# A second buffer for one small exp, and ten more dummy matmuls, in a fused linear attention and MLP

## The chip, the cores and the metric

The kernel runs on one core of a Trainium2 chip. The metric is the device time of one execution in microseconds. TensorE (PE) does matrix products and transposes, ScalarE (ACT) the exp and GELU, VectorE (DVE) the other elementwise work, GpSimd (POOL) some casts and loads, and SyncE (SP) issues most transfers. Each engine works through its own instructions in the order in which they were written, and waits for another engine's semaphore where it needs its data or its buffer. The kernel before took 313.79 us, the median of three runs (313.42 to 314.2).

## The reference

```python
# q, k, v: (8 batches, 8 heads, 576 tokens, 64), float32
phi = lambda x: np.where(x > 0, x, np.exp(x) - 1) + 1      # = max(x, 0) + min(exp(x), 1)
kv  = einsum('bhsd,bhse->bhde', phi(k), v)                 # 64 x 64 per batch and head
z   = sum over the tokens of phi(k)
x   = (phi(q) @ kv) / (phi(q) @ z + 1e-6)                  # attention, all heads side by side: (4608, 512)
h   = x @ w_in                                             # 512 -> 2048
out = gelu_tanh(h) @ w_out                                 # 2048 -> 512, float32
```

## The kernel before

**Tiling.** Of the 576 tokens of a batch, 512 are its main part (128 partitions, 4 tokens each; one set of 128 tokens is called a chunk) and 64 are the rest. The rests of two batches form one group of 128 rows, so there are four groups, m = 0 to 3, of which the tiles are kr, vr and qr (k_r, v_r, q_r when loaded). The MLP runs over nine blocks of 512 tokens: j = 0 to 7 are the main parts, and the ninth is the four groups of rests. For each block `first_half(j)` computes h in 16 column tiles h_ps (L303, four matmuls of 512 columns each) and ScalarE applies GELU to each (L678). `second_half(j)` computes the output in 64 matmuls into four tiles o_ps (L721), which VectorE (L734, even chunks) and ScalarE (L736, odd chunks) copy to o_sb; two stores per block are issued on ScalarE's queue (L652).

**Attention of a batch.** ScalarE takes exp of k, of the resting k, of q and of the resting q (`exp_main` L167, `phi_rest` L189). VectorE makes phi of them (L172, L176) and casts v to vp (L204). PE computes kv_ps (L220, L228) head pair by head pair, five matmuls each; VectorE copies it to kvbd (L244). phi(q) is transposed to qt, by four transposing DMAs on SP's queue (L463, L615) for later batches, and on PE for the first two (L337, L249). Then the products n_ps (L255) follow, one per chunk, VectorE normalises each to x (L265, L267), and x is transposed to xt, either on PE (t_ps, L278, copied by ScalarE, L392) for batches 0, 1 and 2, or by DMA (L498). `first_half(j)` needs the whole of xt of its batch. The rests go the same way in `plan_rest` (qtr L512).

**Order around the change.** Attention of later batches is written into slots of the two MLP halves: `at(phase, j, slot, fn)` puts fn behind the matmuls of that slot. What matters here: in the second half of j = 1, slot 7 has the exps of k and q of batch 3, and then, from the line `at(2, 1, 7, ...)` near the end, the exp of resting q of group 1; slot 12 has the load of the GELU table; slots 13 to 15 have the transposes of batch 2's x on PE with ScalarE's copies to xt, in one order with the o_sb copies of j = 1. On VectorE, the phi of k of batch 3 is in slot 15 of that half; in the first half of j = 2, slot 0 has the cast of v, slot 1 the phi of q (and the transposing DMAs), slot 3 the phi of resting q of group 0, slots 4 to 7 the kv products of batch 3, slot 8 the phi of resting q of group 1, slots 11 to 14 the products with qt, slot 15 those of the resting group and the exps of batch 4. The exp of resting q of group 0 was done on ScalarE at the end of the first half of j = 1, with the exps of batch 2.

**Buffers.** The results of exp lie in the pool `pe` (L47), which has one buffer for each tile name. `phi_rest` (L186) names its tile after the tensor, so all groups of resting q share one tile, qr_e. The loaded q_r tiles lie in a pool with two buffers, as do the phi tiles.

**The first batch.** While its loads and exps run, PE is given dummy matmuls on a tile of zeros: `keep_warm(n)` (L326) issues 2n of them, 252 columns each (L329). The order on PE is: a group of 34, the transposes of the first two head pairs of q (L337), a group of 3, the transposes of the other two, a group of 1, the kv products of batch 0, a group of 1, and then the products and transposes of x with groups of 2 and 1 among them.

Of the kernel before, what the change touches and what calls it, by code (L numbers as in the profile page):

```python
# [9 lines left out]
BF16 = mybir.dt.bfloat16  # L10
# [5 lines left out]
def kernel(  # L16
# [14 lines left out]
    B, H, S, D = q.shape  # L31
    d_model, d_ff = moe_w_in.shape
    P = 128
# [13 lines left out]
    pe = ctx.enter_context(tc.tile_pool(name="pe", bufs=1))  # L47
# [122 lines left out]
    def phi_into(xp, x, e, hs):  # L170

        nc.vector.tensor_scalar(e[:, hs], e[:, hs], 1.0, None, op0=ALU.min)  # L172
        xv = x.rearrange("p h (c d) -> p c h d", d=D)
        ev = e.rearrange("p h (c d) -> p c h d", d=D)
        for c in range(xp.shape[1]):
            nc.vector.scalar_tensor_tensor(  # L176
                xp[:, c, hs, :], xv[:, c, hs, :], 0.0, ev[:, c, hs, :],
                op0=ALU.max, op1=ALU.add,
            )

    def phi_of(x, e, name):
        xp = pphi.tile([P, x.shape[2] // D, H, D], BF16, name=name)
        phi_into(xp, x, e, slice(0, H))
        return xp

    def phi_rest(name, m):  # L186
        x = ld[name, m]
        e = pe.tile([P, H, D], BF16, name=name + "_e")
        nc.scalar.activation(e, x, AF.Exp)  # L189
        return lambda: phi.__setitem__((name, m), phi_of(x, e, name + "_p"))  # L190

# [134 lines left out]
    def keep_warm(n):  # L326
        w_ps = ps_ho.tile([P, 512], FP32, name="w_ps", tag="ho")
        for _ in range(2 * n):
            nc.tensor.matmul(w_ps[:, 0:252], lhsT=warm[:, 0:P], rhs=warm)  # L329
# [3 lines left out]
    def transpose_q(i, copy):  # L333
        src = q_src(0)
        t_ps = ps_ho.tile([P, C, 2, P], BF16, name="t_ps", tag="ho")
        for c in range(C):
            nc.tensor.transpose(t_ps[:, c, 0, :], src(c, i), ident)  # L337
        copy(out=qt[:, :, i, :], in_=t_ps[:, :, 0, :])

    for n, e, s in (  # L340
# [7 lines left out]
            exp_rest_half(n, e, 0)  # L348
        else:
            nc.scalar.activation(e[:, s], ld[n, 0][:, s], AF.Exp)  # L350
    keep_warm(34)
    phi_into(kp, ld["k", 0], ke, halves[0])
    phi_into(kp, ld["k", 0], ke, halves[1])
    phi_into(qp, ld["q", 0], qe, halves[0])
# [1 line left out]
    cast_v(0, nc.scalar.copy, halves[0])  # L356
    for i in range(2):
        transpose_q(i, nc.scalar.copy)
    keep_warm(3)
    phi_into(qp, ld["q", 0], qe, halves[1])  # L360
    cast_v(0, nc.scalar.copy, halves[1])
    ke1 = exp_main("k", 1)
    cast_vr(0, (0,))
    for i in range(2, NP):
        transpose_q(i, nc.vector.tensor_copy)
    keep_warm(1)
    for i in range(NP):
        if i % 2 == 0:
            kv_ps = ps_a.tile([P, 2, 512], FP32, name="kv_ps", tag="a")
# [69 lines left out]
    def plan_prepare(b, exp_at, k_at, kr_at, v_at, q_at, qr_at, table_at):  # L439
# [3 lines left out]
        def exps():  # L443
            box["k"] = exp_main("k", b)
            if b % 2 == 0:
                box["kr"] = phi_rest("kr", b // 2)
            box["q"] = exp_main("q", b)
            if b % 2 == 0:
                box["qr"] = phi_rest("qr", b // 2)
# [143 lines left out]
    def plan_third():  # L593
# [4 lines left out]
        def exps():  # L598
            box["k"] = exp_main("k", b)
            box["kr"] = phi_rest("kr", 1)  # L600
            box["q"] = exp_main("q", b)
            box["qr"] = phi_rest("qr", 0)
            gelu_table()
# [193 lines left out]
```

## Time and profile before

| what | value |
|---|---|
| median of three runs | 313.79 us (313.42 to 314.2) |
| the profiled execution | 316.52 us, span 314.7 us |
| PE busy | 291.0 us, 92% of the span |
| ACT busy | 161.3 us, 51% |
| DVE busy | 132.1 us, 42% |
| POOL busy | 36.9 us, 12% |
| mean granted clock of TensorE | 0.962 |
| chain that ended last | PE 80%, DMA 7%, DVE 5%, ACT 4%, issue 3% |

The profile is of one execution. Busy shares are means over the span; the page also cuts the span into 40 slices of 7.87 us, in which a digit is the busy share in tenths. The chain that ended last is followed back from the last instruction, at each step to what released it. In a timeline a line is an instruction or a run of like ones; the brackets give the idle time of the engine before it and what ended it.

### The profile page before, as it was taken

The numbers are of one execution on the slowest core, as the hardware profiler recorded it, in microseconds if no ns is written. First come the engines' busy times: TensorE is split into PE (matmuls) and PEld (weight loads), VectorE is DVE, ScalarE is ACT, GpSimd is POOL, SyncE is SP. The second block draws the span as 40 slices with busy tenths as digits, with TensorE's granted clock in tenths as the row PEclk, the third lists the DMA queues.
The fourth block names the chain that finished last, engine by engine and source line by source line (L and its number), as shares of the span: only waits on it lengthen the run. The fifth ranks groups of instructions, "written<-read, shape, count | busy, mean of one in ns | idle before, by whom it ended". The sixth has DMA issues, their size and how long they took to land.

```text
span 314.7 us, 4258 instructions
## 1 busy us (share of the span) xinstructions
PE 291.0 (92%) x1651; PEld 150.8 (48%) x1680; DVE 132.1 (42%) x242; ACT 161.3 (51%) x223; POOL 36.9 (12%) x55
## 2 busy tenths in 40 slices
PE   8799999999813999989999999999999999999994
PEld 7566456544501454445445444544454444444443
DVE  3969685208790046924381459236433000000001
ACT  4757834789306468246825682567254036216500
POOL 7039558100005010000000000000000000000000
PEclk9969999999965799999999999999999999999999
DMA  7999899991678214992594468630613110011032
GB/s 247 346 391 390 308 387 338 334 332 27 196 263 210 92 42 93 358 256 55 157 357 123 61 218 307 120 67 28 160 30 69 67 67 0 2 67 67 2 67 68
DMA packets 64260, 53.24 MB, mean 169 GB/s; under 512 B 31728, under 2 KB 57584, under 8 KB 64240
## 3 DMA queue, kind: packets, MB, share of 16 engines
q1 hardware_dynamic: 60816, 41.82, 45.4%
q10 hardware_dynamic: 2464, 8.52, 7.2%
q0 software_dynamic: 960, 2.62, 3.1%
q8 instruction: 13, 0.21, 0.3%
q14 instruction: 7, 0.06, 0.0%
HBM read 36.70 MB, written 9.44 MB: 147 GB/s over the span
## 4 chain that ended last, share of the span: by engine, by line
PE 80%; DMA 7%; DVE 5%; ACT 4%; issue 3%; ACTq 0%; SPq 0%; DVEq 0%
PE h_ps L303 39%; PE o_ps L721 33%; DMA v_x<-in_v_dram 4%; PE n_ps L255 3%; PE kv_ps L220 3%; DMA q_x<-in_q_dram 2%; DVE q_p L176 1%; DMA out_dram<-o_sb 1%; ACT xt L392 1%; PE kv_ps L228 1%; DVE k_p L176 1%; PE w_ps L329 1%; PE t_ps L278 1%; ACT o_sb L736 1%; DVE q_e L172 0%
## 5 line engine op out<-in xcount | busy, mean ns | idle before, releaser
L303 PE MATMUL h_ps<-xt,w_in_sb 128*128 128x512 bf16 (+1 forms) x527 | 121.3, 374 | 3.9 <-ACT xt L392 2.2
L721 PE MATMUL o_ps<-w_out_sb,g 128*128 128x512 bf16 x545 | 123.5, 379 | 1.0 <-ACT w_out_sb L157 0.2
L678 ACT ACTIVATE g<-h_ps 128x512 bf16<-128x512 f32 x144 | 84.2, 598 | 53.0 <-PE h_ps L303 50.8
L303 PEld LDWEIGHTS <-w_in_sb 128*128 128x128 bf16 x604 | 57.8, 99 | 60.4 <-issue 7.3
L721 PEld LDWEIGHTS <-g 128*128 128x128 bf16 x560 | 54.1, 98 | 63.3 <-issue 0.5
L734 DVE COPY o_sb<-o_ps 128x512 f32<-128x512 f32 x17 | 11.7, 688 | 62.4 <-PE o_ps L721 62.3
L736 ACT COPY o_sb<-o_ps 128x512 f32<-128x512 f32 x18 | 10.6, 586 | 52.8 <-PE o_ps L721 52.8
L244 DVE CAST kvbd<-kv_ps 64x260 bf16<-64x260 f32 (+1 forms) x17 | 6.7, 395 | 47.8 <-PE kv_ps L228 47.7
L267 DVE TENSOR_TENSOR x<-n_ps,r 128x512 bf16<-128x512 f32 x36 | 24.9, 692 | 1.2
L176 DVE SCALAR_TENSOR_TENSOR k_p<-k_x,k_e 128x512 bf16<-128x512 f32 (+1 forms) x36 | 23.7, 721 | 0.3
L176 DVE SCALAR_TENSOR_TENSOR q_p<-q_x,q_e 128x512 bf16<-128x512 f32 (+1 forms) x40 | 23.0, 636 | 0.3
L172 DVE TENSOR_SCALAR k_e<-k_e 128x2048 bf16<-128x2048 bf16 (+1 forms) x9 | 5.9, 653 | 29.9 <-ACT k_e L167 25.3
L265 DVE RECIPROCAL r<-n_ps 128x8 f32<-128x8 f32 x36 | 7.4, 206 | 25.8 <-PE n_ps L255 25.8
L278 PE MATMUL t_ps<-ident,x 128*128 128x128 bf16 x48 | 5.3, 240 | 11.2 <-ACT o_sb L736 9.7
L167 ACT ACTIVATE k_e<-k_x 128x2048 bf16<-128x2048 f32 x7 | 13.4, 1910 | 2.1 <-DMA k_x<-in_k_dram 2.1
L255 PEld LDWEIGHTS <-qt 128*128 128x128 bf16 x128 | 10.3, 102 | 7.6 <-issue 1.1
L303 PE MATMUL h_ps<-xt_rest,w_in_sb 128*128 128x512 bf16 x63 | 13.9, 379 | 0.1
L255 PE MATMUL n_ps<-kvbd,qt 128*128 128x130 bf16 x128 | 13.2, 227 | 0.4 <-DVE kvbd L244 0.3
L329 PE MATMUL w_ps<-warm 128*128 128x252 bf16 x84 | 12.5, 310 | 1.1 <-DVE warm L128 1.1
L220 PE MATMUL kv_ps<-vp,k_p 128*128 128x130 bf16 x128 | 13.1, 231 | 0.0
L220 PEld LDWEIGHTS <-k_p 128*128 128x128 bf16 x128 | 10.1, 101 | 5.9
L146 ACT ACT_TABLE_LOAD x8 | 10.3, 1283 | 4.0 <-DVE o_sb L734 3.9
(58 smaller groups left out, 153.3 us busy)
## 6 DMA issues: line engine op xcount, KB each, us to landing
out_dram<-o_sb ACTq DMA_DIRECT2D x16, 512.0 KB, 4.3
k_x<-in_k_dram SPq DMA_DIRECT2D x7, 1024.0 KB, 6.0
v_x<-in_v_dram SPq DMA_DIRECT2D x7, 1024.0 KB, 11.8
q_x<-in_q_dram SPq DMA_DIRECT2D x6, 1024.0 KB, 7.9
w_st<-in_moe_w_out_dram SPq DMA_DIRECT2D x4, 1024.0 KB, 9.7
w_st<-in_moe_w_in_dram SPq DMA_DIRECT2D x3, 1024.0 KB, 9.4
q_x<-in_q_dram SPq DMA_DIRECT2D x4, 512.0 KB, 9.2
k_x<-in_k_dram SPq DMA_DIRECT2D x2, 512.0 KB, 4.1
```

Source lines behind the costliest of these rows:

```text
L146: nc.scalar.preload_act_table_set("gelu_apprx_tanh_and_others")
L167: nc.scalar.activation(e, ld[name, b], AF.Exp)
L176: nc.vector.scalar_tensor_tensor(xp[:, c, hs, :], xv[:, c, hs, :], 0.0, ev[:, c, hs, :], op0=ALU.max, op1=ALU.add,)
L220: nc.tensor.matmul(dst, lhsT=kp[:, c, P * i : P * (i + 1)], rhs=vps[b % 2][:, 2 * i : 2 * i + 2, c, :], start=(c == 0), stop=False,)
L255: nc.tensor.matmul(n_ps[rows, i // 2, 2 * E * (i % 2) : 2 * E * (i % 2) + 2 * E], lhsT=qt_c[:, i, rows], rhs=kvbd[:, i, :], skip_group_che ...
L267: nc.vector.tensor_tensor(x, n_v[:, :, :, 0:D], r[:, :, :, None].to_broadcast([P, 2, 4, D]), op=ALU.mult,)
L303: nc.tensor.matmul(h_ps[:, tok], lhsT=w_in_sb[:, c, P * m : P * (m + 1)], rhs=xt[:, c, tok], start=(c == 0), stop=(c == KM - 1), skip_grou ...
L329: nc.tensor.matmul(w_ps[:, 0:252], lhsT=warm[:, 0:P], rhs=warm)
L678: nc.scalar.activation(gs[j][:, i, :], ps, AF.Gelu_apprx_tanh)
L721: nc.tensor.matmul(o_pss[t], lhsT=g[:, m, P * t : P * (t + 1)], rhs=w_out_sb[:, m, :], start=(m == 0), stop=(m == MM - 1),)
L734: nc.vector.tensor_copy(dst, o_ps)
L736: nc.scalar.copy(dst, o_ps)
```

## The change

`phi_rest` names the exp tile of resting q after the parity of its group, qr_e0 or qr_e1; the name for resting k stays kr_e. Three calls of `keep_warm` in the first batch have larger counts: 34 becomes 36, 3 becomes 5, and 1 becomes 2 (the one ahead of the kv products of batch 0), which is ten matmuls of 252 columns more.

```diff
--- before.py
+++ after.py
@@ -185,7 +185,7 @@
 
     def phi_rest(name, m):
         x = ld[name, m]
-        e = pe.tile([P, H, D], BF16, name=name + "_e")
+        e = pe.tile([P, H, D], BF16, name=f"{name}_e{m % 2 if name == 'qr' else ''}")
         nc.scalar.activation(e, x, AF.Exp)
         return lambda: phi.__setitem__((name, m), phi_of(x, e, name + "_p"))
 
@@ -348,7 +348,7 @@
             exp_rest_half(n, e, 0)
         else:
             nc.scalar.activation(e[:, s], ld[n, 0][:, s], AF.Exp)
-    keep_warm(34)
+    keep_warm(36)
     phi_into(kp, ld["k", 0], ke, halves[0])
     phi_into(kp, ld["k", 0], ke, halves[1])
     phi_into(qp, ld["q", 0], qe, halves[0])
@@ -356,14 +356,14 @@
     cast_v(0, nc.scalar.copy, halves[0])
     for i in range(2):
         transpose_q(i, nc.scalar.copy)
-    keep_warm(3)
+    keep_warm(5)
     phi_into(qp, ld["q", 0], qe, halves[1])
     cast_v(0, nc.scalar.copy, halves[1])
     ke1 = exp_main("k", 1)
     cast_vr(0, (0,))
     for i in range(2, NP):
         transpose_q(i, nc.vector.tensor_copy)
-    keep_warm(1)
+    keep_warm(2)
     for i in range(NP):
         if i % 2 == 0:
             kv_ps = ps_a.tile([P, 2, 512], FP32, name="kv_ps", tag="a")
```

## Rows read from the trace of the kernel before

**Rows 1.** Page, 40 slices of the span: busy tenths of PE, and granted clock.
```profile
PE   8799999999813999989999999999999999999994
...
PEclk9969999999965799999999999999999999999999
```

**Rows 2.** Timeline of ScalarE, 79 to 101 us: start, duration, operation, count [idle before].
```profile
79.57 1.89 ACT L167 ACTIVATE q_e<-q_x 128x2048 bf16<-128x2048 f32 x1
94.61 0.63 ACT L189 ACTIVATE qr_e<-q_r 128x512 bf16<-128x512 f32 x1 [13.14 <-DVE qr_p L176]
...
97.16 0.34 ACTq L652 DMA_DIRECT2D out_dram<-o_sb  x1
...
98.50 0.60 ACT L736 COPY o_sb<-o_ps 128x512 f32<-128x512 f32 x1
```

**Rows 3.** Timeline of VectorE, the last phi of batch 3's work.
```profile
93.88 0.69 DVE L176 SCALAR_TENSOR_TENSOR qr_p<-q_r,qr_e 128x512 bf16<-128x512 f32 x1
```

**Rows 4.** Timeline of TensorE, 86 to 101 us.
```profile
86.29 0.38 PE L278 MATMUL t_ps<-ident,x 128*128 128x128 bf16 x4 [0.78 <-DVE o_sb L734]
86.51 1.03 PE L721 MATMUL o_ps<-w_out_sb,g 128*128 128x512 bf16 x4
...
100.65 0.59 PE L303 MATMUL h_ps<-xt,w_in_sb 128*128 128x512 bf16 x1 [1.88 <-ACT xt L392]
```

**Rows 5.** Chain that ended last, h_ps of batch 2: start, duration, what, count.
```profile
101.45 6.59 PE h_ps L303 x18
...
108.33 0.86 PE h_ps L303 x4
```

**Rows 6.** Windows of TensorE: length, busy (count), granted clock, DMA share, GB/s.
```profile
4.00:4.50 0.50, 0.50 (x5) 1.00 1.08 383
4.50:5.00 0.50, 0.50 (x7) 1.00 1.09 387
...
11.00:14.00 3.00, 2.02 (x15) 1.00 1.12 353
14.00:14.50 0.50, 0.34 (x3) 0.91 1.08 385
...
89.00:90.00 1.00, 0.00 (x0) 0.75 1.08 385
106.00:107.00 1.00, 1.00 (x4) 0.71 0.00 0
```

**Rows 7.** Tile q_r, 45 to 60 us: count, durations in ns, first and last start.
```profile
L76 POOL DMA_DIRECT2D q_r<-in_q_dram x4: 682/682/684, 49.5 to 51.5; - x4
```

**Rows 8.** Tile qt, 85 to 120 us: issues as in rows 7, and landing.
```profile
L463 SPq DMA_TRANSPOSE qt<-q_p x4: 1190/1216/1217, 91.9 to 95.8; - x4
...
DMA to landing us min/median/max: 2.3/3.0/4.7
```

**Rows 9.** Timeline of TensorE in the first batch.
```profile
11.96 0.81 PE L329 MATMUL w_ps<-warm 128*128 128x252 bf16 x6
13.39 1.72 PE L337 MATMUL t_ps<-ident,q_p 128*128 128x128 bf16 x8 [0.61 <-DVE q_p L176]
```

**Rows 10.** Chain that ended last: first batch, then kv of batch 1.
```profile
15.11 0.42 PE w_ps L329 x2
...
18.48 0.54 PE w_ps L329 x2
...
47.72 0.23 PE kv_ps L220 x4
```

**Rows 11.** Chain that ended last, 124 to 138 us.
```profile
124.87 13.03 DMA v_x<-in_v_dram
137.99 0.35 ACTq L652
```

**Rows 12.** Timeline of SyncE's queue, a load of batch 4.
```profile
82.36 1.26 SPq L67 DMA_DIRECT2D v_x<-in_v_dram  x1
```

**Rows 13.** Tile v_x, 20 to 160 us: landing of six loads.
```profile
DMA to landing us min/median/max: 9.7/12.4/17.4
```

## The prediction, made before the change was run

> **What bounds the kernel now.** I read the page's 40 slices first. PE is busy in nearly all of them and stands at 9 tenths or so to the end: after the first hundred microseconds the kernel is bound by TensorE's stream of matmuls [rows 1]. Two places break this. At about 87 to 102 us PE falls to 0 and 1 tenths and the granted clock to 5, and near 16 to 24 us the clock reads 6 while PE is busy (the two levels are 1.00, 2.4 GHz, and 0.50, 1.2 GHz; a slice between is a mean). What comes after is paced by PE, so time taken out of either place should reach the end.
>
> For the large hole I read ScalarE's timeline. It ends the exp of q of batch 3 at 81.46, then waits 13.14 us, until VectorE has finished qr_p, before a 0.63 us exp into qr_e; all that stands behind it in ScalarE's order waits too: a table load, the copy of o_sb, a store, the copies of xt [rows 2]. The qr_p waited for is the phi of the *first* group of resting q, 93.88 to 94.57, the last of VectorE's work for batch 3 [rows 3]. VectorE does not wait for ScalarE there; it is busy with that batch. So the wait is for the buffer qr_e: the exp of the second group may not overwrite the first group's before VectorE has read it.
>
> PE shows the price. Its last product of batch 1 ends at 87.54 and h_ps of batch 2 starts at 100.65, with only eight transposes between [rows 4]. That start is slow too: 18 matmuls take 6.59 us, against 0.86 for four later [rows 5], because the clock fell at about 89.5 and rose at about 106.6 [rows 6].
>
> **The second qr_e buffer.** It adds no instruction and removes none. Group m writes qr_e0 or qr_e1, so the exp at 94.61 no longer depends on the phi of group 0. Its input is no obstacle: the loads of q_r for both groups were issued from 49.5 to 51.5 [rows 7], 30 us ahead. Later groups meet a buffer whose phi ran two groups back, long done.
>
> Step by step. From the start of this exp to the o_sb copy of chunk 3 ScalarE took 98.50 - 94.61 = 3.89 us, all serial [rows 2]. Started at 81.50 it would be there at 85.4, so from now on PE holds it: the second set of transposes still waits for VectorE's copy of o_sb and ends at 86.67, and the last product of chunk 3 ends at 87.54 [rows 4]. From there the old pieces follow: 98.50 to 100.65 is 2.15 us for this o_sb copy, a store, two xt copies and the hand-over to PE. So h_ps starts at 87.54 + 0.04 (the hand-over) + 2.15 = 89.7 instead of 100.65: 10.95 us earlier. What is late next is this tail; the last two sets of transposes, 0.2 us each, run right behind 87.54, and PE then rests about 1.7 us.
>
> Does the rest follow? Phi, casts and transposes of batch 3 stay where they are, since VectorE was never held, but they are needed sooner. The kv products of batch 3 come after five groups of h_ps, 89.7 + 5 x 0.86 = 94.0; k_p and vp lie ahead of the qr_p that starts at 93.88 on VectorE [rows 3]. The products with qt come after 12 groups and four kv's of 0.29: 101.2. The transposing DMAs for them are issued at 91.9 to 95.8 and land within 4.7 us [rows 8]: the first by 96.6, the last by 100.5 with need at about 104.5. That cover of 4 us hides them; beyond it each microsecond of delay costs one. The loads of batch 4 now meet the two stores, 1 MB more at the 385 GB/s of the row of 89 to 90 [rows 6], 2.6 us: these loads are wanted only at the end of that h_ps stage, past 105, and the 2.6 us are inside the cover of 4.
>
> The clock: at full speed the 19 matmuls from 100.65 to 108.04 would take 19 x 0.215 = 4.1 instead of 7.4 us [rows 5], so up to 3.3 us come back. How much is the main uncertainty, as the new stop of 1.7 us might itself lose the clock. Bounds: nothing lost, or all 3.3. When PE goes dense at once with the clock down, the nearest row is the kernel's start: matmuls begin near 1.05 and their count per half microsecond goes from 5 to 7 at 4.5 [rows 6], so some 3.4 us at half speed (the clock's column shows 1.00 there all the same), a loss of 1.7. I take that if it falls. Would it? Before the fall at 14.4, PE was busy for 2.02 of the 3.00 us from 11 to 14 [rows 6], in pieces, with no stop over about 0.6 us [rows 9]. The new tail is emptier: a stop of 0.78, four products and twelve transposes, a stop of 1.7. By these rows it falls.
>
> The Trainium skill reads otherwise: "TensorE: Matmul & The Clock Gate", section "HAM oscillation — how this bites in real kernels", ties the fall to TensorE standing idle between bursts, and stops of 0.6 us would hardly count as that. By that rule the time is rival 1's, by the trace the forecast's; the fall at 14.4 speaks against the rule.
>
> Sum for this part: 10.95 + 3.3 - 1.7 = 12.55 us (without a new fall 14.25, with one as dear as the old 10.95).
>
> **The dummy matmuls.** keep_warm(n) issues 2n: four more in the first group, four in the second, two in the third. A group of six takes 0.81 us; taking 0.27 for the last, a step of one is 0.54 / 5 = 0.108, so four add 0.43. The second group's fall into the 0.61 us that PE waits for q_p ahead of 13.39 [rows 9]; the first group's into a like wait ahead of 10.67. Both are hidden, since VectorE's q_p sets those starts; if q_p came 0.4 earlier they would cost up to 0.4 each.
>
> The third is on the path, ahead of kv. If the clock falls at 14.4 as before, two more cost what two cost now, 0.42. If the filling keeps it up, four take 4 x 0.108 = 0.43, as two did, and the four kv's, 2.95 us from 15.53 to 18.48, take what they take in batch 1 at full speed, 0.23 for four matmuls and so 0.29 for five [rows 10]: 4 x 0.29 = 1.17, a gain of 1.8 that VectorE's chain behind it can follow whole. So -0.4 to +1.8. Neither end is nearer: little idle is left beside the dummies, but the transposes still come singly, at q_p's pace. I take the middle, 0.7.
>
> **Sum.** 12.55 + 0.7 = 13.25 us. The profiled execution took 316.52, its span 314.7 and 1.8 around it; the median of the timed runs, 313.79, is 2.7 below. I take the sum off the median: 300.5 (profiled, about 303.3).
>
> **Rivals.**
> 1. The wait goes and the clock holds over the new tail: 14.25 + 0.7 = 14.95, time 298.8. For it: PE is dense up to 85.5 and again from 89.7. Against it: the fall at 14.4.
> 2. The wait moves to a store. At 137.99 ScalarE issues a store only once v_x, issued at 124.87, has landed 13.03 us later [rows 11]; in the program's order that store is the eighth transfer after this v_x on the SP and ACT queues (four qt, a store, two qtr, this store). If the first store of batch 1, now ready at about 85, stood so behind batch 4's v_x, issued at 82.36 [rows 12], then with the shortest landing of a v_x, 9.7 us [rows 13], it would go out at 92.1 instead of 97.16 [rows 2]: 5.1 us gained, 308.7. With the longest, 17.4, it goes out at 99.8, 2.6 us later than before: 316.4, slower. It decides from a landing of 14.8. Against it: counted the same way, this store's eighth predecessor is a store of batch 0, landed long since.
> 3. The exp still waits, for something else that VectorE's last phi stands for: then only the dummies act, 313.1 (312.0 to 314.2). Against it: the two share nothing else.
> 4. The next stage meets late transposes: a delay of 7 us instead of the 4 that are covered gives 3 back, 303.5.
>
> **Chances.** Forecast 0.46, rival 1 0.40, rival 2 0.05, rival 3 0.03, rival 4 0.06. The forecast's own range is 299.4 to 303.2 (dummies +1.8 to -0.4, clock loss 1.7 to 3.3); rival 1 spans 297.7 to 299.9. The range 297.8 to 302.8 leaves out the tails and rivals 2 to 4. About 0.3% is what a measurement can tell from no change. Faster: the forecast, rivals 1 and 4, most of 2, some of 3: 0.95. Same: the middle of rival 3, 0.02. Slower: the long landings of rival 2, and the rest of rival 3, 0.03.
>
> **What would show it.** ScalarE's exp into the second qr_e directly behind that of q at about 81.5; PE's hole cut to about 1.7 us and h_ps of batch 2 starting near 89.7 (near 88 if the first batch gains its 1.8). The granted clock in the microseconds after 89 tells the forecast from rival 1; the clock between 14.5 and 21, and kv at 0.29 or 0.74 us a piece, tell the dummies' sign. The prediction is wrong if ScalarE waits elsewhere between 82 and 88, or if a new PE wait stands ahead of the kv or qt products of batch 3.

## The result, and the profile after

The changed kernel takes 298.94 us, the median of four runs (298.67 to 299.23), against 314.0 us for the kernel before (313.42 to 316.13): a ratio of 0.9509, with a 95% interval from 0.9463 to 0.9555. That is 15.1 us less. The forecast was 300.5 in a range from 297.8 to 302.8; the time lies in the range, and at the first rival's 298.8. Two runs that fell in a slower state of the chip, one of e1 (380.16 us at a mean granted clock of 0.75) and one of the kernel before in the same set (317.08), are left out of the figures below.

The page's 40 slices of the kernel after answer to [rows 1]. The two low slices of PE, whose digits are 1 and 3 there (the prediction read 0 and 1), are gone, and the granted clock reads 9 throughout.

```profile
PE   8989999999979999999999999999999999999994
...
PEclk9999999999999999999999999999999999999999
```

ScalarE's timeline after, the answer to [rows 2] (start, duration, operation, count, idle before). The exp into the second qr_e follows the exp of q at once, and nothing waits 13 us; the copy of o_sb of chunk 1 now waits for PE, and no longer stands behind an exp that waits for VectorE.

```profile
77.54 1.89 ACT L167 ACTIVATE q_e<-q_x 128x2048 bf16<-128x2048 f32 x1
79.34 0.61 ACT L189 ACTIVATE qr_e<-q_r 128x512 bf16<-128x512 f32 x1
...
82.19 0.59 ACT L736 COPY o_sb<-o_ps 128x512 f32<-128x512 f32 x1 [0.94 <-PE o_ps L721]
...
84.60 0.59 ACT L736 COPY o_sb<-o_ps 128x512 f32<-128x512 f32 x1 [0.28 <-PE o_ps L721]
```

VectorE's last phi of batch 3, the answer to [rows 3], starts at 91.84 against 93.88: VectorE's work stands where it stood but for the 2.04 us that the first batch gave. The wait was not shifted to VectorE; it fell away. (The first row is VectorE's copy of o_sb of chunk 2, which is needed further down.)

```profile
83.51 0.69 DVE L734 COPY o_sb<-o_ps 128x512 f32<-128x512 f32 x1
...
91.84 0.69 DVE L176 SCALAR_TENSOR_TENSOR qr_p<-q_r,qr_e 128x512 bf16<-128x512 f32 x1
```

TensorE's timeline after, the answer to [rows 4]. The second set of transposes, 83.31, has no stop ahead of it (0.78 us before), the last product ends at 84.56, the last eight transposes run behind it, and the stop ahead of h_ps of batch 2 is 1.71 us.

```profile
83.31 0.39 PE L278 MATMUL t_ps<-ident,x 128*128 128x128 bf16 x4
83.53 1.03 PE L721 MATMUL o_ps<-w_out_sb,g 128*128 128x512 bf16 x4
84.40 0.61 PE L278 MATMUL t_ps<-ident,x 128*128 128x128 bf16 x8
86.72 4.48 PE L303 MATMUL h_ps<-xt,w_in_sb 128*128 128x512 bf16 x19 [1.71 <-ACT xt L392]
```

The chain that ended last, the answer to [rows 5]: 18 matmuls of h_ps take 4.05 us instead of 6.59, at 0.86 for four from the start.

```profile
87.15 4.05 PE h_ps L303 x18
...
91.49 0.86 PE h_ps L303 x4
```

PE's dearest waits in the whole span after (in total, times, longest): 1.7 us is the tail of batch 1, 1.1 the start of the kernel, and the rest is below a microsecond each.

```profile
PE h_ps L303 <- ACT xt L392: 2.1, 2, 1.7
PE w_ps L329 <- DVE warm L128: 1.1, 1, 1.1
PE t_ps L278 <- DVE x L267: 0.6, 2, 0.4
```

Read against the profile before, the gain comes in five places. The two profiles differ by 17.8 us (316.52 to 298.75), the medians by 15.1; that is taken up below.

| point on PE | before | after | earlier by | new at this point |
|---|---|---|---|---|
| first h_ps of batch 0 | 22.80 | 20.76 | 2.04 | 2.04, first batch |
| first transposes of x of batch 2 | 84.26 | 82.23 | 2.03 | none |
| end of the last o_ps of batch 1 | 87.54 | 84.56 | 2.98 | 0.95, of which 0.78 is PE's stop for VectorE's o_sb |
| first h_ps of batch 2 | 100.65 | 86.72 | 13.93 | 10.95, ScalarE's wait |
| first kv of batch 3 | 108.04 | 91.20 | 16.84 | 2.91, the clock behind the wait |
| end of the span | 314.7 | 297.0 | 17.7 | 0.9, of which 0.80 is one PE wait for a gelu near 139 |

The last place is the wait of [rows 11]. ScalarE's timeline after still shows the store issued late, at 120.26, though the o_sb copy ahead of it ended at 117.70, and the next gelu held up by v_x; but PE no longer waits for that gelu (its list of waits has no such row). This wait varies from profile to profile, 0.80 and 0.21 us in the two of the kernel before, 0.32 in e1 and 0.51 in e10, which have the second buffer, and none in the two of the changed kernel; that the change takes it away is not shown.

```profile
120.26 0.34 ACTq L652 DMA_DIRECT2D out_dram<-o_sb  x1
120.64 2.56 ACT L678 ACTIVATE g<-h_ps 128x512 bf16<-128x512 f32 x5 [2.95 <-DMA v_x<-in_v_dram]
```

### The profile page after: what moved, and what is told of

The parts are those of the page before. It is cut to its first block, busy times and chain, and to the rows that moved or that the text cites. A ratio compares the mean times of both kernels' runs of the same rounds, so it can differ in the third digit from the quotient of the medians.

```text
span 297.0 us, 4281 instructions
## 1 busy us (share of the span) xinstructions
PE 286.2 (96%) x1661; PEld 149.4 (50%) x1690; DVE 131.9 (44%) x242; ACT 161.3 (54%) x223; POOL 37.3 (13%) x55
## 4 chain that ended last, share of the span: by engine, by line
PE 89%; DMA 3%; DVE 3%; ACT 2%; issue 1%; SPq 1%; ACTq 0%; DVEq 0%
PE h_ps L303 42%; PE o_ps L721 40%; PE n_ps L255 3%; PE kv_ps L220 3%; DMA k_r<-in_k_dram 3%; DMA out_dram<-o_sb 1%; PE kv_ps L228 1%; DVE x L267 1%; SPq L67 1%; DVE kvbd L244 1%; ACT xt L392 1%; PE t_ps L278 1%; DVE q_p L176 0%; ACT o_sb L736 0%; ACT w_out_sb L157 0%
## 5 line engine op out<-in xcount | busy, mean ns | idle before, releaser
L303 PE MATMUL h_ps<-xt,w_in_sb 128*128 128x512 bf16 (+1 forms) x527 | 118.5, 367 | 2.7 <-ACT xt L392 2.1
L303 PEld LDWEIGHTS <-w_in_sb 128*128 128x128 bf16 x604 | 57.0, 97 | 57.2 <-issue 2.3
L329 PE MATMUL w_ps<-warm 128*128 128x252 bf16 x94 | 13.6, 308 | 1.1 <-DVE warm L128 1.1
L167 ACT ACTIVATE k_e<-k_x 128x2048 bf16<-128x2048 f32 x7 | 13.4, 1910 | 2.0 <-DMA k_x<-in_k_dram 2.0
L303 PE MATMUL h_ps<-xt_rest,w_in_sb 128*128 128x512 bf16 x63 | 13.9, 379 | 0.1
L220 PEld LDWEIGHTS <-k_p 128*128 128x128 bf16 x128 | 9.5, 97 | 5.6
L220 PE MATMUL kv_ps<-vp,k_p 128*128 128x130 bf16 x128 | 12.2, 220 | 0.0
L150 POOL CAST w_in_sb<-w_st 128x1024 bf16<-128x1024 f32 x8 | 10.1, 1288 | 14.2 <-DMA w_st<-in_moe_w_in_dram 14.2
```

Source lines behind the costliest of these rows:

```text
L167: nc.scalar.activation(e, ld[name, b], AF.Exp)
L220: nc.tensor.matmul(dst, lhsT=kp[:, c, P * i : P * (i + 1)], rhs=vps[b % 2][:, 2 * i : 2 * i + 2, c, :], start=(c == 0), stop=False,)
L303: nc.tensor.matmul(h_ps[:, tok], lhsT=w_in_sb[:, c, P * m : P * (m + 1)], rhs=xt[:, c, tok], start=(c == 0), stop=(c == KM - 1), skip_grou ...
```

## The experiments

Each was run beside the kernel before on the same chip. Ratios are to that kernel in the same set of runs. The edits are shown against the changed kernel, that of e3 against the kernel before.

**e1, the buffer alone.**

```diff
-    keep_warm(36)
+    keep_warm(34)
...
-    keep_warm(5)
+    keep_warm(3)
...
-    keep_warm(2)
+    keep_warm(1)
```

> The second qr_e buffer alone, dummy matmuls at 34, 3, 1 as before. Theory: the buffer takes ScalarE's wait away by itself, and the dummies are worth about 2 us only because they keep the clock up in the first batch. Then ScalarE's exp into the second qr_e follows the exp of q at once, PE's stop ahead of h_ps of batch 2 is about 1.7 us as in the changed kernel, and the time is 301.0 (298.9 + 2.0). Rival, the dummies give nothing in the timed runs: 298.9 to 299.1. Rival, the clock falls again in the tail of batch 1 once the first batch is slow: about 302.7. In all three the h_ps stage of batch 2 starts some 12 us earlier than before relative to the last o_ps of batch 1.

Measured: 300.72 us, the median of five runs (299.86 to 301.91), ratio 0.9551 (0.9508 to 0.9595), so 13.9 us of the change come from this line alone (314.6 for the kernel before in this set). TensorE's timeline of this kernel has the same tail as the changed one, 2.3 us later: no stop ahead of the second set of transposes, 1.72 us ahead of h_ps, and h_ps at full speed. The clock did not fall in the tail.

```profile
85.62 0.39 PE L278 MATMUL t_ps<-ident,x 128*128 128x128 bf16 x4
...
86.71 0.61 PE L278 MATMUL t_ps<-ident,x 128*128 128x128 bf16 x8
89.03 4.48 PE L303 MATMUL h_ps<-xt,w_in_sb 128*128 128x512 bf16 x20 [1.72 <-ACT xt L392]
```

In the first batch of this profile the clock was down (window of TensorE: length, busy, granted clock, DMA share, GB/s), and this run took 301.43 us against the 301.0 expected for that. By the mean granted clock of each run the five split into two groups: 299.86 to 300.72 us at 0.993 to 1.000, and 301.43 and 301.91 at 0.986 and 0.985.

```profile
14.50:17.50 3.00, 2.93 (x20) 0.50 1.12 323
```

**e2, the dummies alone.**

```diff
-        e = pe.tile([P, H, D], BF16, name=f"{name}_e{m % 2 if name == 'qr' else ''}")
+        e = pe.tile([P, H, D], BF16, name=name + "_e")
```

> The ten dummy matmuls alone, one qr_e buffer. Theory: the clock stays at 1.00 in the first batch (kv 0.5 us a piece instead of 0.77), everything behind it comes 2.0 us earlier, ScalarE's wait of 13.1 us for qr_p stays: 312.0 against 314.0. Rival, the dummies only fill idle time and the clock does not depend on them: 314.0, or 314.2 with the third group on the path. If this run is 2 us faster and the run with the buffer alone is 13 us faster, the two parts add up to the measured 15.

Measured: 313.4 us, ratio 0.9973 (0.9945 to 1.0), 1.2 us less than 314.6 and less than the 2 expected; the interval reaches up to no change. With 13.9 it makes the 15.1 of both. PE's waits in this kernel still have ScalarE's o_sb, and beside it the stop of 0.8 for VectorE's o_sb.

```profile
PE t_ps L278 <- ACT o_sb L736: 9.6, 1, 9.6
...
PE t_ps L278 <- DVE o_sb L734: 0.8, 1, 0.8
```

Behind that wait the clock is down here too, but h_ps of batch 2 loses less than in the kernel before (chain that ended last):

```profile
99.19 5.94 PE h_ps L303 x20
```

The clock was up in the first batch.

```profile
14.50:17.50 3.00, 2.89 (x32) 1.00 1.12 339
```

**e3, one buffer, read earlier.**

```diff
-        at(1, 2, 3, lambda: box["qr"]())
+        at(2, 1, 0, lambda: box["qr"]())
```

> One qr_e buffer and the dummies as before, but VectorE's phi of the first group of resting q moved from slot 3 of the first half of j = 2 to slot 0 of the second half of j = 1, right behind the other phi's of batch 2, where VectorE has time. Theory: the wait is for the buffer, so reading it earlier is worth as much as a second one: the same time as the kernel with the buffer alone within 0.5 us (about 301). Rival, the wait stood for something else that VectorE does last: 314. Rival, the buffer gives its gain by the other order of PSUM banks that comes with it: then this kernel, if its banks stand as before, gains about 1 us less.

Measured: 302.0 us, ratio 0.9583 (0.9539 to 0.9626). The wait goes without any second buffer, once VectorE reads the only one before ScalarE needs it again; ScalarE's timeline shows the exp directly behind that of q. So the wait was for the buffer.

```profile
77.89 1.90 ACT L167 ACTIVATE q_e<-q_x 128x2048 bf16<-128x2048 f32 x1
79.69 0.61 ACT L189 ACTIVATE qr_e<-q_r 128x512 bf16<-128x512 f32 x1
...
86.19 0.59 ACT L736 COPY o_sb<-o_ps 128x512 f32<-128x512 f32 x1 [0.28 <-PE o_ps L721]
```

The transposes of x have no stop for VectorE's o_sb here either, though the change of buffers was not made: the stop goes with ScalarE's wait, not with the second buffer. This kernel is 1.3 us slower than e1, more than the 0.5 expected. Four of its six runs have a mean granted clock of 0.989 (301.72 to 303.15 us), two of 0.998 and 0.999 (300.44 and 300.69), against two of five in e1 at the lower clock, which makes up part of the difference. Its profile, of the run of 300.44, has one wait that e1's has not, 1.07 us of PE for a qt of batch 2 (first row below), which landed up to 5.4 us after its issue instead of 2.4; why, the profile doesn't show, and what the other runs have beside the lower clock stays open.

```profile
83.57 0.41 PE L255 MATMUL n_ps<-kvbd,qt 128*128 128x130 bf16 x4 [1.07 <-DMA qt<-q_p]
83.81 0.38 PE L278 MATMUL t_ps<-ident,x 128*128 128x128 bf16 x4
...
84.90 0.39 PE L278 MATMUL t_ps<-ident,x 128*128 128x128 bf16 x4
```

**e4, filling the tail.**

```diff
+        def early(m):
+            first_mm_early(2, m)
...
-            (tx, 1, 14), (tx, 2, 15), (tx, 3, 15),
+            (tx, 1, 14), (tx, 2, 15), (early, 0, 15), (early, 1, 15), (tx, 3, 15),
+            (early, 2, 15),
```

> The changed kernel, and in the second half of j = 1 the first 256 tokens of three h_ps tiles of batch 2 are computed ahead of the last transposes of x (as batch 1 has it already): 12 matmuls of 256 columns, 12 x 0.108 = 1.3 us, moved into the 1.7 us that PE stands still ahead of h_ps of batch 2. Theory: that stop is the dearest one left, so 297.6 to 297.9 against 298.9. Rival, the three tiles find no free PSUM bank before the o_ps copies are done, so PE waits for ScalarE in another place: 298.9 or slower, up to 300.

Measured: 298.38 us, ratio 0.9477 (0.9432 to 0.9522), 0.6 us less than the changed kernel's 298.94 and 1.5 less than the 299.91 of its second set of runs (e5), neither of them in the same set. The stop is down from 1.71 to 0.35, as expected, but in the profiled run, which took 299.51, 0.93 us came back at another place: PE now reaches the products of the resting group before their transposed q has landed.

```profile
85.75 1.04 PE L303 MATMUL h_ps<-xt,w_in_sb 128*128 128x256 bf16 x8
86.62 0.39 PE L278 MATMUL t_ps<-ident,x 128*128 128x128 bf16 x4
87.36 3.68 PE L303 MATMUL h_ps<-xt,w_in_sb 128*128 128x256 bf16 x24 [0.35 <-ACT xt L392]
...
103.56 0.43 PE L255 MATMUL n_ps<-kvbd,qtr 128*64 128x130 bf16 x8 [0.93 <-DMA qtr<-qr_p]
```

**e5, the changed kernel again.** No edit.

> The changed kernel once more, so that the next ones are compared with it on one chip: 298.5 to 299.5, and a ratio to the kernel before of 0.950 to 0.953. Theory of the first batch: the dummies only make a fall of the clock less likely, and the kernel before has runs with and without one, which is why its times spread from 312.3 to 317.1; then this kernel, in which no fall is seen, spreads by less than 2 us.

Measured: 299.91 us (299.0 to 300.74), ratio 0.9537 (0.9487 to 0.9586), beside a kernel before of 314.82 (312.35 to 316.82). The expected spread holds, 1.7 us against 4.5; the median is 0.4 above what was expected, and the ratio, 0.9537, just above its range too.

**e6, filling the tail and moving the resting group.**

```diff
-    plan_rest(0, (1, 2, 3), 2, 15)
+    plan_rest(0, (1, 2, 3), 3, 0)
```

This is e4 with that line.

> The changed kernel with three half tiles of h_ps of batch 2 ahead of the last transposes, and the products of the first resting group moved from slot 15 of the first half of j = 2 to slot 0 of that of j = 3, because with the half tiles alone PE came to those products 0.9 us before qtr had landed. Theory: the 1.3 us that the half tiles gain are then kept: 1.2 to 1.4 us faster than the changed kernel, about 297.6. Rival: the products moved meet another wait 14 us later (a PSUM bank, or the kv copy of batch 4), and the gain stays at the 0.5 us seen with the half tiles alone: 298.4.

Measured: 298.07 us (297.44 to 299.22), ratio 0.9484 (0.9439 to 0.9528), 1.8 us less than the changed kernel in the same set of runs (299.91, lowest 299.0). The ranges of the runs overlap by 0.2 us. Its median is the lowest of all; by the ratio it is level with e4 (0.9477), so that the line moved gains anything beyond e4 is not shown. PE no longer waits for qtr, and its wait for xt is 0.7 us in two pieces instead of 2.1:

```profile
PE h_ps L303 <- ACT xt L392: 0.7, 2, 0.3
```

**e7 and e8, a longer tail.** ScalarE's last xt copy of batch 2 is done 4 times (e7, as below) and 8 times (e8).

```diff
+        def copies(out, in_):
+            for _ in range(4):
+                nc.scalar.copy(out=out, in_=in_)
...
-            pe_tx(b, c, box["x", c], True)
+            pe_tx(b, c, box["x", c], True, copies if c == 3 else nc.scalar.copy)
```

> The changed kernel with ScalarE's last xt copy of batch 2 done four times instead of once, so that PE's stop ahead of h_ps of batch 2 grows from 1.7 to about 3.2 to 3.5 us. Theory: the clock held in the changed kernel because the stop was short; at this length it may hold still: 300.5 (298.9 + 1.6) if it holds, 302.2 to 303.5 if it falls, since the h_ps matmuls behind it then run at half speed for 3.4 to 6 us. Rival: the clock goes by what stands around the stop as well (as in the fall at 14.4, with no stop over 0.6 us), and falls here though it held at 1.7.

Measured: 301.49 us in one run. PE's stop is 3.56 us, and h_ps behind it runs at full speed, 19 matmuls in 4.48 us as in the changed kernel. The clock held, in this one run.

```profile
89.47 4.48 PE L303 MATMUL h_ps<-xt,w_in_sb 128*128 128x512 bf16 x19 [3.56 <-ACT xt L632]
```

> The same with eight copies instead of one: a stop of 5.0 to 5.8 us. Theory: a stop as long as this loses the clock, as the one of 9.65 us did: 302.6 (298.9 + 3.7) plus 1.7 to 3.0 for h_ps at half speed, 304.3 to 305.6, with granted clock 0.50 behind the stop. Rival: the clock holds even here, so that only the very long wait of the kernel before lost it: 302.6.

Measured: 307.28 us in one run. The stop is 6.04 us and 18 matmuls take 6.62 us, against 4.05: the clock fell. TensorE's windows show it on the way from 1.00 to 0.50 in the microsecond from 90, still in the stop, and on the way back in the one from 97.

```profile
91.66 0.58 PE L303 MATMUL h_ps<-xt,w_in_sb 128*128 128x512 bf16 x1 [6.04 <-ACT xt L632]
92.46 6.62 PE L303 MATMUL h_ps<-xt,w_in_sb 128*128 128x512 bf16 x18 [0.22 <-issue]
```

```profile
90.00:91.00 1.00, 0.00 (x0) 0.92 1.08 424
...
97.00:98.00 1.00, 1.00 (x4) 0.67 1.16 190
```

Against e5's 299.91 the 7.4 us are 4.33 of stop (6.04 - 1.71) and 2.9 of h_ps at half speed (from its start at 91.66 to the first kv behind it, 99.08, 7.42 instead of the 4.48 from 86.72 to 91.20). So the fall cost 2.9 us behind this stop, in one run.

**e9 and e10, which dummies.** Both have the second buffer. e9 has no dummies in the second and third group, e10 only the second group enlarged.

```diff
-    keep_warm(36)
+    keep_warm(34)
...
-    keep_warm(5)
...
-    keep_warm(2)
```

This is e9's; e10's keeps the 5 and has 1 for the 2.

> The second qr_e buffer, and in the first batch no dummies at all in the second and third group (34, 0, 0 instead of 34, 3, 1). Theory: the dummies among the transposes of q are what keeps the granted clock up to the kv products; without any, it falls at about 14 in every run, kv takes 0.77 us a piece and the time is as in the runs of the buffer alone that fell, 301.1 to 301.9. Rival: whether the clock falls there is a matter of the run and hardly of the dummies; then 299.5 to 300.5, as for the changed kernel.

Measured: 301.15 us (299.24 to 302.21), ratio 0.9586 (0.9551 to 0.9621). The clock fell in the profiled run. The runs spread over 3 us, and the lowest is as fast as kernels in which it held. Yet the mean granted clock of all six is 0.986 to 0.991, against 0.997 to 1.000 in every run of the changed kernel: the clock was lower in every run, as expected, and the spread in time has another source beside it, which stays open.

```profile
14.50:17.50 3.00, 2.89 (x24) 0.56 1.12 329
```

> The second qr_e buffer, and of the dummies only the second group enlarged (34, 5, 1). Theory: this group alone fills the stop ahead of the second pair of transposes, in which the clock was lost; so the clock holds as in the changed kernel, the time is 299.5 to 300.0, and the other two groups give nothing. Rival: it takes the first group too (the end of the warm-up), and this kernel still falls in some runs: about 300.5.

Measured: 299.59 us, all runs from 299.49 to 299.99, ratio 0.9551 (0.9525 to 0.9577), 1.6 us less than e9 in the same set. The clock held in the profiled run, and the mean granted clock of all five runs is 1.000.

```profile
14.50:17.50 3.00, 2.94 (x31) 1.00 1.15 340
```

**e11, the kernel before, a second profile.** No edit.

> The kernel before once more, for a second profile. Theory: its times from 312.3 to 317.1 differ by whether the clock falls in the first batch (about 2 us) and by how long after the 13 us wait h_ps runs at half speed (up to 3.3 us). So this profile either shows the fall at 14.4 and a time above 314.5, or no fall and a time near 313.

Measured: 314.08 us, span 312.3. The clock did not fall in the first batch; the time is a microsecond above the 313 named. This run was emptier than that of [rows 6], where the clock fell: PE was busy for 1.68 us of the 3 from 11 to 14 (2.02 there), with a stop of 1.04 us (0.61 there). The last row, from the chain that ended last, is h_ps of batch 2 behind the long wait.

```profile
11.00:14.00 3.00, 1.68 (x14) 1.00 1.13 327
14.50:17.50 3.00, 2.84 (x29) 1.00 1.13 308
```

```profile
99.50 6.74 PE h_ps L303 x20
```

Over all profiles the fall goes with the second group: where it has 3 or none the clock fell in the first batch in three (before, e1, e9) and held in two (e3, e11); where it has 5 it held in all eight (after, e2, e4, e5, e6, e7, e8, e10). The first h_ps of batch 0 starts at 22.66 to 23.07 where it fell and at 20.73 to 21.89 in the ten where it held, e3 (20.73) and e11 (21.36) among them: the first batch is as fast with few dummies as with more, if the clock holds.

## Why the prediction came out as it did

**The wait (right).** The step "h_ps starts at 89.7 instead of 100.65: 10.95 us earlier" measured 10.95 from the end of the last product of batch 1: 2.16 with the last transposes and the stop of 1.71, against 13.11. Two runs show that the cause is the buffer: e1 with a second one, e3 with the same one read earlier.

**The tail (a term missed).** "The second set of transposes still waits for VectorE's copy of o_sb" failed. In the program before, these transposes wait for VectorE's o_sb (0.78 us) and the third set for ScalarE's (9.65). In the changed one the second set starts at 83.31, ahead of VectorE's copy at 83.51, so it can't wait for it. e2 (ScalarE's wait kept, the stop kept) and e3 (the wait gone, one buffer, the stop gone) tie the stop to the wait. It is worth 0.95 us. That the two sets have exchanged their PSUM banks, and that the banks of `ps_ho` are handed out by an estimate of which is free first, in which a stuck ScalarE comes last, would explain it; this is argued, not shown.

**The clock in the tail (wrong, and the largest error of the sum).** The step "By these rows it falls" failed: with a stop of 1.71 us the clock held in every trace (after, e1, e3, e5, e9, e10), and in e7 at 3.56. It fell at 6.04 (e8) and in the wait of 9.6 where the buffer was not changed (before, e2, e11). I had read the fall at 14.4 as if a quieter stretch must always do it, but that fall does not come in every run: the unchanged kernel shows it in one profile of two, and the emptier of the two is the one in which the clock held (e11). The Trainium skill, "TensorE: Matmul & The Clock Gate", section "HAM oscillation — how this bites in real kernels", has the clock go with longer stops between bursts of matmuls. The stops of 1.71, 6.04 and 9.65 us agree with that; for the 3.56 of e7, which held, it can be read either way, and the run decides. The fall in the first batch, with no stop over 0.62 us in the profile before, does not agree.

**What the old fall gave back (mis-sized).** What a fall costs also varies: the five groups of h_ps ahead of the first kv take 4.48 us at full speed, and took 7.4 in the kernel before and in e8, 6.7 in e11 and 5.9 in e2, a loss of 2.9, 2.3 and 1.5 us. The 1.7 read from the kernel's start lies among these, but the 3.3 put down for the old fall was more than any profile had to give back: it counted the 19 matmuls that the trace before shows, where five groups of four are 20 (e1's row above has them all). Without a fall the forecast had 14.25 for the buffer; e1 measured 13.9, which is what 10.95, the 0.95 of the tail and a gain of 1.5 to 2.9 from the clock make (13.4 to 14.8). That the time meets rival 1's 298.8 to 0.1 us is thus partly luck: the term it lacked and the term it had too large partly cancel.

**The dummies (right in sign, the parts off).** The sum had +0.7 between -0.4 and +1.8; e2 measured 1.2, with an interval that reaches nothing. In e10 the second group alone held the clock in all five runs, but its ratio, 0.9551, is also e1's, so a gain in time over the old groups is not shown for it. The changed kernel's first batch shows why the detail was off.

```profile
11.27 0.61 PE L337 MATMUL t_ps<-ident,q_p 128*128 128x128 bf16 x8
11.72 1.24 PE L329 MATMUL w_ps<-warm 128*128 128x252 bf16 x10
13.07 1.46 PE L337 MATMUL t_ps<-ident,q_p 128*128 128x128 bf16 x8
...
14.80 0.40 PE L220 MATMUL kv_ps<-vp,k_p 128*128 128x130 bf16 x4
```

```profile
11.00:14.00 3.00, 2.64 (x26) 1.00 1.13 322
14.50:17.50 3.00, 2.79 (x29) 1.00 1.13 332
```

In this profile the first group ran past q_p: there is no wait ahead of 11.27, so it did delay these transposes, at no cost. That is more than its four dummies, since the group took 10.38 us here and 9.75 in e5, the same kernel, which still waited 0.28 us for q_p. The second nearly fills its gap (busy 2.64 of the 3 us from 11 to 14, against 2.02), and the third is on the path. A kv takes 0.50 us (14.80 to the next at 15.29), not the 0.29 taken from batch 1: its fifth matmul has only 64 rows here (L228) and starts 0.33 us behind the first instead of 0.24, and the next kv 0.16 behind it instead of 0.05. With the clock down it is 0.77. In one profile the first batch gains 2.04 us; over runs the gain is smaller, as the kernel before loses the clock there in only some of them.

**The base (a choice that mattered).** The sum was made against the profiled execution and taken off the median. The profiled execution, at 316.52, was one with every loss at once: the fall in the first batch, the longest half-speed stretch, the PE wait of 0.80. e11, without the first, with less of the second and 0.2 of the last, has a span of 312.3. So the profiles say 17.8 and the medians 15.1.

**Late transposes and the store (rivals 2 and 4).** The store was not held behind batch 4's v_x: it went out at 82.81, behind its o_sb copy, while that v_x, issued at 80.33, landed 14.8 us later. The transposes of q for batch 3 now take 5.0 to 5.8 us to land against 2.3 to 4.7 in [rows 8]; the last, issued at 94.7, is there by 100.5 and needed at 101.5. So the cover of 4 us was used down to 1, at no cost; for the resting group it is used up, with a PE wait of 0.34 us in e5 and 0.93 in e4.

```profile
L463 SPq DMA_TRANSPOSE qt<-q_p x4: 1207/1216/2124, 89.9 to 94.7; - x4
...
DMA to landing us min/median/max: 5.0/5.4/5.8
```

## What to carry to other kernels

When an engine stands still, look at whom it waits for and then at what that one frees: here a 1 KB buffer per partition, read last in a long row of work on another engine, cost 13 us, and either a second buffer or an earlier read takes it away. ScalarE ran its instructions in order, so count what stands behind the waiting one. The short stops here cost only themselves, and the long ones twice, once as a stop and once as half speed behind it; and where a profile shows a loss that only some runs have, take its worth from several runs.

## What the runs showed that was not expected

- PE's second set of transposes lost a stop of 0.78 us for VectorE's copy though no line about either was changed; that another order of PSUM banks is the reason is not shown.
- The same program loses the clock in its first batch in some executions and not in others; the times of the kernel before spread from 312.3 to 316.8 us over all sets, those of e10 from 299.49 to 299.99.
- Stops of 1.71 and 3.56 us between dense stretches kept the granted clock at 1.00 (2.4 GHz); one of 6.04 us was followed by 0.50 (1.2 GHz), at a cost of 2.9 us; behind the same wait of 9.6 us three profiles lost 1.5, 2.3 and 2.9 us.
